# A sigmoid gate computed as one more column of a k projection and carried to its layout through DRAM

## The chip, the cores and the metric

The kernel runs on one core of a Trainium2 chip. The core has a matrix engine (TensorE, in the profile PE, with its weight loads as PEld), a vector engine (VectorE, DVE), an activation engine (ScalarE, ACT), a general engine (GpSimd, POOL) and a queue engine (SyncE, SP) that here only issues DMAs. The metric is the device time of one execution in microseconds, as the median of three runs.

## The reference

Two linear-attention blocks A and B, with weights of their own, read the same x (2048 rows, 640 columns, bf16). A gate mixes their outputs row by row:

```python
x = A_x
g = sigmoid((x * gate_w).sum(-1, keepdims=True))   # one number for each row of x
qkv = x @ wqkv                                      # 640 -> 3 * 640, 32 heads of 20
phi = lambda t: where(t > 0, t + 1, exp(t)) + 1e-6
pq, pk = phi(q), phi(k)
kv  = einsum("bhsd,bhse->bhde", pk, v);  z = einsum("bhsd->bhd", pk)
o   = einsum("bhqd,bhde->bhqe", pq, kv) / (einsum("bhqd,bhd->bhq", pq, z) + 1e-6)
a   = o @ wo            # and b in the same way with B's weights
out = g * a + (1 - g) * b
```

The gate's logit of a row is a dot product of that row with gate_w. With e the exponential of the logit, 1 / g is 1 + 1 / e and 1 / (1 - g) is 1 + e.

## The kernel before

The rows of x are cut into 16 chunks of 128 (ST = 16, half of them hc = 8), its 640 columns into 5 blocks of 128 (DT = 5). xT holds x transposed, xn holds x as it is. The first 512 rows come in by four loads and are transposed on PE (x_transpose, L207); the other 1536 rows are transposed by 15 DMA transposes on SP's queue (L155). DMAs are issued from SP and, for three blocks of x, one block of wkA and two late outputs, from ACT.

The program is written out by hand in the order in which each engine issues its work (`tc.manual_schedule`). The framework adds the waits between engines. PSUM tiles of the first stage go through four slots of two banks each, in turn.

In the first stage k of A is computed chunk by chunk: k_chunk (L258) multiplies a chunk of xT by wkA in two halves of 320 columns, 5 matmuls each, and k_done applies phi: an exponential on ACT (L225), a clamp on DVE (L230) and a combining operation on DVE that reads PSUM (L239). k_first (L265) does this for the first four chunks, interleaved with the transposes of x, so that work starts as blocks of x and of wkA land. The q projection comes in between as q_block and q_unit (L305), 10 matmuls of 512 columns each.

After the last k chunk q_pass (L743) runs the second half of q for A. Behind its first unit stands the gate's pass (gate_pass, L198): 40 matmuls of 256 columns. Its weights, gwr, are the gate column repeated 32 times, so that the logits appear in the layout of the denominators: 32 equal partitions for each of four groups of 256 rows, two halves side by side. ACT takes two exponentials of them (L204) and DVE adds one and clamps (L205): geA is 1 / g and geB is 1 / (1 - g). gate_w itself comes by a DMA of 640 single elements (gcol, L776). z_rows (L510) then sums pk over the rows.

rec_pass (L573) multiplies the denominators by ge on DVE and takes reciprocals (L582, L587). norm_spread (L623) spreads these over the heads by matmuls (exA), and q is scaled by them. So the gate reaches A's and B's q through the reciprocal. The rest of the kernel computes the summed products of pk and x (gs, gA), the same for B, and the outputs by Strassen-like products. The change doesn't touch it.

The program order of SP's queue matters: after the transposes it holds gcol, three loads of xn, wvA, woA and its rest, wkB (which goes to wkA's place and so waits until A's last k chunk is done), and wqB (which waits for A's last q).

```python
gate_pass()                                    # L747, behind the first q unit of the second half
in1=ge[b][:, part], op0=ALU.add, op1=ALU.mult  # L583, the gate's first use
k_chunk(0, ST - 2)                             # L789
nc.vector.tensor_copy(out=gwr[:], ...)         # L791
k_chunk(0, ST - 1)                             # L792
```

Of the kernel before, what the change touches and what calls it, by code (L numbers as in the profile page):

```python
# [8 lines left out]
P = 128  # L9
FP32 = mybir.dt.float32  # L10
BF16 = mybir.dt.bfloat16
# [5 lines left out]
DT = D // P  # L17
# [15 lines left out]
def kernel(  # L33
# [66 lines left out]
    ones = persist.tile([P, H], BF16, name="ones")  # L100
    gwr = persist.tile([P, DT, H], BF16, name="gwr")
    hc, ic = ST // 2, 2 * P
# [18 lines left out]
    )]  # L121
    ge = [persist.tile([P, 2 * RB], FP32, name=f"ge{b}") for b in "AB"]

# [10 lines left out]
    wq = [None, None]  # L134
    wk[0] = wpool.tile([P, DT, D], BF16, tag="wk", name="wkA")
    def load_x(eng, lo, hi):
        eng.dma_start(out=xn[:, lo:hi, :], in_=xb0[:, lo:hi, :])

    def load_wk(eng, lo, hi):
        eng.dma_start(out=wk[0][:, lo:hi, :], in_=wq_dram[0][:, lo:hi, D:2 * D])  # L140
# [10 lines left out]
    nc.sync.dma_start(out=wq[0][:], in_=wq_dram[0][:, :, 0:D])  # L151
    gcol = persist.tile([P, DT], BF16, name="gcol")
    for n in range(1, NB):
# [43 lines left out]

    def gate_pass():  # L198

        pt = ps("lg")  # L200
        for h in range(2):
            by_group(pt[:, 0, h * RB:(h + 1) * RB], gwr, xT, h)
        for b in range(2):
            nc.scalar.activation(out=ge[b][:], in_=pt[:, 0, :], func=ACT.Exp, scale=(-1.0, 1.0)[b])  # L204
            nc.vector.tensor_scalar(ge[b][:], ge[b][:], 1.0, 1e30, op0=ALU.add, op1=ALU.min)  # L205

    def x_transpose(i, slot, eng, cuts=(0, DT)):  # L207
        pt = ps_raw("xt", slot)
        for c in range(DT):
            nc.tensor.transpose(out=pt[:, c * P:(c + 1) * P], in_=xn[:, i, c * P:(c + 1) * P], identity=ident[:])  # L210
        copy = nc.scalar.copy if eng == "act" else nc.vector.tensor_copy
        src = pt[:, 0:D].rearrange("p (c n) -> p c n", c=DT)
        for lo, hi in zip(cuts, cuts[1:]):
            copy(out=xT[:, lo:hi, i * P:(i + 1) * P], in_=src[:, lo:hi])

    class Phi:
# [31 lines left out]

    def k_mm(b, i, c, pt, hf):
        nc.tensor.matmul(  # L250
            pt[:, hf, 0:HF], lhsT=xT[:, c, i * P:(i + 1) * P], rhs=wk[b][:, c, hf * HF:(hf + 1) * HF],
            start=(c == 0), stop=(c == DT - 1),
        )

    def k_done(b, i, pt):
        phi(pk[:, i, :].rearrange("p (b n) -> p b n", b=2), pt[:, :, 0:HF])

# [7 lines left out]
    def k_first():  # L265

        pts = [ps("kA", (2 + i) % 4) for i in (0, 1)]

        def part(i, cs):
            for c in cs:  # L270
                for hf in range(2):
# [12 lines left out]
        for i in range(3):  # L284
            part(i, (3, 4))
            k_done(0, i, pts[i])
        k_chunk(0, 3, 0)

# [284 lines left out]
    def rec_pass(b, zsel, slot):  # L573
# [5 lines left out]
        for h in range(2):  # L579
            part = slice(h * RB, (h + 1) * RB)  # L580
            d1 = work.tile([P, RB], FP32, tag="d1", name="d1")
            nc.vector.scalar_tensor_tensor(  # L582
                out=d1[:], in0=pt[:, 0, part], scalar=EPS, in1=ge[b][:, part], op0=ALU.add, op1=ALU.mult  # L583
            )
            rT = work.tile([P, RB], BF16, tag="rT", name="rT")
            with nc.allow_low_precision(reason="a fp32 reciprocal, stored as the bf16 that multiplies bf16"):
                nc.vector.reciprocal(out=rT[:], in_=d1[:])  # L587
            rts.append(rT)
# [173 lines left out]
    with tc.manual_schedule():  # L762
# [12 lines left out]
    with nc.allow_non_contiguous_dma(reason="640 elements, one to a partition and column"):  # L775
        nc.sync.dma_start(out=gcol[:], in_=gate_w.rearrange("(c p) -> p c", p=P))  # L776
    for n in range(1, NB):
# [4 lines left out]
    load_wo(0, nc.sync)  # L782
    wk[1] = load_w(1, "k", nc.sync)

# [3 lines left out]
    with tc.manual_schedule():  # L788
        k_chunk(0, ST - 2)  # L789
        turn[0] = (turn[0] + 1) % 4  # L790
        nc.vector.tensor_copy(out=gwr[:], in_=gcol[:, :, None].to_broadcast([P, DT, H]))  # L791
        k_chunk(0, ST - 1)  # L792
        k_sum(0, 1)
        zsel = q_pass([(m, 1) for m in range(DT)])
# [69 lines left out]

        scratch = ctx.enter_context(tc.tile_pool(name="scratch", bufs=1, space=bass.MemoryType.DRAM))
        m_rows = scratch.tile([D, D], BF16, name="m_rows")

# [144 lines left out]
```

## Time and profile before

| | |
|---|---|
| runs | 189.8, 189.89, 190.78 us; median 189.89 us |
| profiled execution | 191.16 us, its span 189.4 us, granted clock 1.0 |
| PE, PEld | 184.4 us (97%), 123.6 us (65%) |
| DVE, ACT, POOL | 156.0 us (82%), 86.7 us (46%), 8.6 us (5%) |
| chain: PE, DMA, DVE, ACT | 91%, 3%, 2%, 1% |
| DMA | 15.64 MB in 19759 packets |

The profile is one execution, and its times are positions in its span in microseconds. "L250" is line 250 of the kernel; a helper's line covers all its callers, so tile names tell more: kA is k of A in PSUM, lg the gate's logits, denA the denominators, d and rT their product with the gate and its reciprocal, exA the spread reciprocals. A row of the timeline gives start, length, engine, line, operation, what is written from what, shape and count, and in brackets how long the engine stood before it and for whom. The chain is the work that ended last, followed back. Rows of windows give, for a stretch, the busy time of each engine, then the clock, the DMA engines' share and GB/s.

### The profile page before, as it was taken

To read this page: it belongs to the slowest core of one execution; us is meant where nothing else is said; L and a number is where in the kernel's file an instruction comes from. 1 tells how busy PE (TensorE), PEld (TensorE's weight loads), DVE (VectorE), ACT (ScalarE), POOL (GpSimd) and SP (SyncE) were. 2 spreads that over 40 slices of the span, in tenths; PEclk is the share of its full clock that TensorE was granted. 3 is DMA by queue.
4 is the path that set the end of the run, shared out by engine and by line. 5 is a ranking of instruction groups with operands and counts; after the bars stand their busy time and mean duration, and the time that the engine had idled before them with its cause. 6 is when DMAs were issued, how large, how long until landed. Compare 5 with 4: busy or idle time off the path is not lost.

```text
span 189.4 us, 3688 instructions
## 1 busy us (share of the span) xinstructions
PE 184.4 (97%) x1494; PEld 123.6 (65%) x1494; DVE 156.0 (82%) x267; ACT 86.7 (46%) x134; POOL 8.6 (5%) x23
## 2 busy tenths in 40 slices
PE   8899999999999999999999999999999999999992
PEld 3566657766567677676666665767677776777771
DVE  1368968999898999998898987999997989787553
ACT  2055478544963351563959685662611611111110
POOL 8900000000000000000000000000000000000000
PEclk9999999999999999999999999999999999999999
DMA  6984439992040000005000000146600003213112
GB/s 181 321 147 88 105 61 315 324 194 106 3 143 31 3 0 0 0 3 165 8 3 2 0 0 0 29 137 214 146 0 3 0 3 108 99 39 106 69 69 71
DMA packets 19759, 15.64 MB, mean 83 GB/s; under 512 B 9502, under 2 KB 19614, under 8 KB 19742
## 3 DMA queue, kind: packets, MB, share of 16 engines
q1 hardware_dynamic: 18878, 14.59, 28.0%
q10 hardware_dynamic: 864, 0.82, 1.3%
q8 instruction: 11, 0.18, 0.4%
q14 instruction: 6, 0.05, 0.1%
HBM read 10.00 MB, written 3.44 MB: 71 GB/s over the span
## 4 chain that ended last, share of the span: by engine, by line
PE 91%; DMA 3%; DVE 2%; ACT 1%; ACTq 0%; issue 0%; DVEq 0%
PE gs L453 16%; PE qA L294 11%; PE kA L250 11%; PE kB L250 11%; PE q L348 7%; PE ox L653 6%; PE oy L653 5%; PE oz L653 5%; DMA xn<-in_A_x_dram 3%; PE ow L653 3%; PE gB L424 2%; PE gA L424 2%; PE qB L294 1%; PE q L294 1%; DVE osb L658 1%; PE mA L872 1%
## 5 line engine op out<-in xcount | busy, mean ns | idle before, releaser
L250 PEld LDWEIGHTS <-xT 128*128 128x128 bf16 x320 | 31.4, 99 | 15.0 <-issue 0.2
L230 DVE TENSOR_SCALAR e<-e 128x640 bf16<-128x640 bf16 (+2 forms) x56 | 19.3, 344 | 6.9 <-ACT e L225 6.7
L250 PE MATMUL kB<-wkB,xT 128*128 128x320 bf16 x160 | 24.2, 299 | 0.0
L250 PE MATMUL kA<-wkA,xT 128*128 128x320 bf16 x160 | 23.4, 306 | 0.0
L294 PE MATMUL qA<-xT,wqA 128*128 128x512 bf16 x100 | 22.4, 379 | 0.0
L294 PEld LDWEIGHTS <-wqA 128*128 128x128 bf16 x100 | 11.6, 118 | 9.3 <-issue 0.3
L225 ACT ACTIVATE e<-kA 128x640 bf16<-128x640 f32 x16 | 11.1, 704 | 13.3 <-PE kA L250 13.2
L453 PEld LDWEIGHTS <-xn 128*128 128x128 bf16 x128 | 12.2, 98 | 5.2 <-issue 0.5
L225 ACT ACTIVATE e<-kB 128x640 bf16<-128x640 f32 x16 | 11.3, 708 | 9.0 <-PE kB L250 8.9
L239 DVE SCALAR_TENSOR_TENSOR pk<-kA,e 128x640 bf16<-128x640 f32 x16 | 13.2, 824 | 1.7
L239 DVE SCALAR_TENSOR_TENSOR pk<-kB,e 128x640 bf16<-128x640 f32 x16 | 13.2, 823 | 1.5
L225 ACT ACTIVATE e<-qA 128x1024 bf16<-128x1024 f32 x10 | 10.2, 1024 | 8.6 <-PE qA L294 8.1
L697 ACT COPY u<-ox 128x320 f32<-128x320 f32 x8 | 3.4, 426 | 21.9 <-PE ox L653 21.9
L225 ACT ACTIVATE e<-q 128x512 bf16<-128x512 f32 x18 | 10.8, 598 | 5.4 <-PE q L348 3.8
L653 PEld LDWEIGHTS <-xT 128*128 128x128 bf16 x85 | 8.0, 98 | 3.0 <-DVE xT L592 0.2
L653 PEld LDWEIGHTS <-pqTA 128*128 128x128 bf16 x85 | 7.9, 98 | 2.9 <-issue 0.2
L653 PEld LDWEIGHTS <-pqTB 128*128 128x128 bf16 x80 | 7.8, 98 | 3.0
L453 PE MATMUL gs<-pk,xn 128*128 128x320 bf16 x64 | 9.5, 299 | 0.0
L348 PE MATMUL q<-xT,wqB 128*128 128x512 bf16 x32 | 9.5, 379 | 0.0
L658 DVE TENSOR_TENSOR osb<-oz,u 128x320 bf16<-128x320 f32 (+1 forms) x18 | 8.0, 452 | 1.6 <-PE oz L653 0.9
L424 PEld LDWEIGHTS <-xn 128*128 128x128 bf16 x64 | 6.3, 98 | 3.0 <-issue 0.4
L681 ACT COPY p1s<-ox 128x320 f32<-128x320 f32 x8 | 3.4, 426 | 10.0 <-PE ox L653 10.0
(145 smaller groups left out, 319.5 us busy)
## 6 DMA issues: line engine op xcount, KB each, us to landing
out_dram<-osb SPq DMA_DIRECT2D x14, 160.0 KB, 1.8
xn<-in_A_x_dram SPq DMA_DIRECT2D x3, 640.0 KB, 6.7
wqA<-in_A_wqkv_dram SPq DMA_DIRECT2D x1, 800.0 KB, 6.6
wvA<-in_A_wqkv_dram SPq DMA_DIRECT2D x1, 800.0 KB, 10.3
wkB<-in_B_wqkv_dram SPq DMA_DIRECT2D x1, 800.0 KB
wqB<-in_B_wqkv_dram SPq DMA_DIRECT2D x1, 800.0 KB, 4.5
wvB<-in_B_wqkv_dram SPq DMA_DIRECT2D x1, 800.0 KB, 4.5
MA<-m_rows SPq DMA_DIRECT2D x1, 800.0 KB, 4.5
```

The lines of the kernel that those rows point to most:

```text
L225: nc.scalar.activation(out=to, in_=part, func=ACT.Exp)
L230: nc.vector.tensor_scalar(self.e, self.e, 1.0, EPS, op0=ALU.min, op1=ALU.add)
L239: nc.vector.scalar_tensor_tensor(out=dst, in0=src, scalar=1.0 + EPS, in1=e, op0=ALU.add, op1=ALU.max)
L250: nc.tensor.matmul(pt[:, hf, 0:HF], lhsT=xT[:, c, i * P:(i + 1) * P], rhs=wk[b][:, c, hf * HF:(hf + 1) * HF], start=(c == 0), stop=(c == D ...
L294: nc.tensor.matmul(dst, lhsT=mixed(wq[b][:, c, :], m), rhs=xT[:, c, n * HB:(n + 1) * HB], start=first, stop=last,)
L348: nc.tensor.matmul(dst, lhsT=left(c), rhs=right(c), start=first and k == 0, stop=k == len(cs) - 1, skip_group_check=not first,)
L424: nc.tensor.matmul(pt[:, hf, 0:HF], lhsT=xn[:, i, c * P:(c + 1) * P], rhs=pk[:, i, hf * HF:(hf + 1) * HF], start=(i == 0), stop=(i == ST - 1),
L453: nc.tensor.matmul(pt[:, n, 0:HF], lhsT=left[:, i, n * P:(n + 1) * P], rhs=right[:, i, :], start=(first and i == 0), stop=(i == hc - 1), s ...
L653: nc.tensor.matmul(dst, lhsT=left[:, c, r0:r0 + P], rhs=right[:, c, :], start=(first and c == 0), stop=(c == DT - 1), skip_group_check=not ...
L658: nc.vector.tensor_tensor(out=dst, in0=acc, in1=sb, op=ALU.add)
L681: nc.scalar.copy(out=self.p1s[:], in_=self.at("x"))
L697: nc.scalar.copy(out=self.u2[:], in_=self.at("x"))
```

## The change

Four things change.

The gate's logits become a 641st column of A's k. wkA gets 642 columns, of which 640 are loaded as before. gate_w comes as 5 rows of 128 (g5), is transposed on PE into a free part of the PSUM tile of the second transposed chunk, and is copied by DVE into column 640 of each of the 5 blocks (gate_column). The second half of each of A's k chunks is then 321 columns wide, and k_done takes one more exponential on ACT, of that single column, into gl (128 partitions, 16 columns).

The gate's pass on PE, its two exponentials, its two DVE operations, gwr and gcol go. Instead gate_rows makes 1 + 1 / e and 1 + e for eight chunks at a time with three small DVE operations; gate_store writes them to a DRAM tile in row order, element by element, 2048 elements a time; gate_load reads them back, four DMAs a half, each to 32 partitions with the row repeated, into one tile ge for both blocks.

On SP's queue g5's load stands before wkA's third block; gcol is gone; wkB comes after the two stores and before the eight loads.

k_first has a new order: first-half products of chunk 0 for blocks 0 and 1, the gate's column, those of chunk 1, the second halves, both chunks' block 2 and only then the transpose of x's third block; the third and fourth chunks run as plain k chunks at the end.

```diff
+    g5 = persist.tile([DT, P], BF16, name="g5")
+    gl = persist.tile([P, ST], FP32, name="gl")
+    gf = persist.tile([P, 2, 2, ST // 2], FP32, name="gf")
...
-    ge = [persist.tile([P, 2 * RB], FP32, name=f"ge{b}") for b in "AB"]
+    ge = persist.tile([P, 2, 2 * RB], FP32, name="ge")
+    g_rows = [scratch.tile([2, SH], FP32, name=f"g_rows{h}") for h in range(2)]
...
-    wk[0] = wpool.tile([P, DT, D], BF16, tag="wk", name="wkA")
+    wk[0] = wpool.tile([P, DT, D + 2], BF16, tag="wk", name="wkA")
...
     load_wk(nc.scalar, 1, 2)
+    nc.sync.dma_start(out=g5[:], in_=gate_w.rearrange("(c p) -> c p", p=P))
     load_wk(nc.sync, 2, 3)
...
-    def gate_pass():
-        pt = ps("lg")
-        for h in range(2):
-            by_group(pt[:, 0, h * RB:(h + 1) * RB], gwr, xT, h)
-        for b in range(2):
-            nc.scalar.activation(out=ge[b][:], in_=pt[:, 0, :], func=ACT.Exp, scale=(-1.0, 1.0)[b])
-            nc.vector.tensor_scalar(ge[b][:], ge[b][:], 1.0, 1e30, op0=ALU.add, op1=ALU.min)
+    def gate_column(pt):
+        nc.tensor.transpose(out=pt[:, 2 * HB:2 * HB + DT], in_=g5[:], identity=ident[0:DT, 0:DT])
+        nc.vector.tensor_copy(out=wk[0][:, :, D:D + 1], in_=pt[:, 2 * HB:2 * HB + DT, None])
+
+    def gate_rows(h):
+        cols = slice(h * ST // 2, (h + 1) * ST // 2)
+        nc.vector.tensor_scalar(gf[:, h, 1], gl[:, cols], 1e-30, 1e30, op0=ALU.max, op1=ALU.min)
+        nc.vector.reciprocal(out=gf[:, h, 0], in_=gf[:, h, 1])
+        nc.vector.tensor_scalar(gf[:, h], gf[:, h], 1.0, 1e30, op0=ALU.add, op1=ALU.min)
+
+    def gate_store(h):
+            nc.sync.dma_start(out=g_rows[h].rearrange("b (i p) -> p (b i)", p=P), in_=gf[:, h].rearrange("p b i -> p (b i)"))
+
+    def gate_load(h):
+        for j in range(4):
+            nc.sync.dma_start(
+                out=ge[32 * j:32 * j + 32, :, h * RB:(h + 1) * RB],
+                in_=g_rows[h][None, :, j * RB:(j + 1) * RB].to_broadcast([H, 2, RB]),
+            )
...
     def k_mm(b, i, c, pt, hf):
+        n = HF + (b == 0 and hf == 1)
         nc.tensor.matmul(
-            pt[:, hf, 0:HF], lhsT=xT[:, c, i * P:(i + 1) * P], rhs=wk[b][:, c, hf * HF:(hf + 1) * HF],
+            pt[:, hf, 0:n], lhsT=xT[:, c, i * P:(i + 1) * P], rhs=wk[b][:, c, hf * HF:hf * HF + n],
...
     def k_done(b, i, pt):
-        phi(pk[:, i, :].rearrange("p (b n) -> p b n", b=2), pt[:, :, 0:HF])
+        f = Phi(pk[:, i, :].rearrange("p (b n) -> p b n", b=2), pt[:, :, 0:HF])
+        if b == 0:
+            nc.scalar.activation(out=gl[:, i:i + 1], in_=pt[:, 1, HF:HF + 1], func=ACT.Exp)
+        f.clamp()
+        f.top()
...
         for i in range(2):
-            x_transpose(i, i, "dve", (0, 2, DT))
+            pt = x_transpose(i, i, "dve", (0, 2, DT))
+        part(0, (0, 1), (0,))
+        gate_column(pt)
+        part(1, (0, 1), (0,))
         for i in range(2):
-            part(i, (0, 1))
-        x_transpose(2, 0, "dve", (0, 2, DT))
+            part(i, (0, 1), (1,))
         for i in range(2):
             part(i, (2,))
-        pts.append(ps("kA", 1))
-        part(2, (0, 1, 2))
-        x_transpose(3, 0, "dve")
-        for i in range(3):
-            part(i, (3, 4))
+        x_transpose(2, 0, "dve", (0, 2, DT))
+        part(0, (3, 4))
+        x_transpose(3, 1, "dve", (0, 2, DT))
+        part(1, (3, 4))
+        for i in range(2):
             k_done(0, i, pts[i])
-        k_chunk(0, 3, 0)
+        for i in (2, 3):
+            k_chunk(0, i, i - 2)
...
-                out=d1[:], in0=pt[:, 0, part], scalar=EPS, in1=ge[b][:, part], op0=ALU.add, op1=ALU.mult
+                out=d1[:], in0=pt[:, 0, part], scalar=EPS, in1=ge[:, b, part], op0=ALU.add, op1=ALU.mult
...
         q_unit(0, *units.pop(0))
-        gate_pass()
         zr = z_rows(0)
...
-        nc.sync.dma_start(out=gcol[:], in_=gate_w.rearrange("(c p) -> p c", p=P))
...
-    wk[1] = load_w(1, "k", nc.sync)
...
         k_chunk(0, ST - 2)
         turn[0] = (turn[0] + 1) % 4
-        nc.vector.tensor_copy(out=gwr[:], in_=gcol[:, :, None].to_broadcast([P, DT, H]))
+        gate_rows(0)
+        gate_store(0)
         k_chunk(0, ST - 1)
+        gate_rows(1)
+        gate_store(1)
+        wk[1] = load_w(1, "k", nc.sync)
+        for h in range(2):
+            gate_load(h)
         k_sum(0, 1)
```

More of the change, by code (lines that the diff above doesn't have):

```diff
@@ L121 @@
     )]
-    ge = [persist.tile([P, 2 * RB], FP32, name=f"ge{b}") for b in "AB"]
+    ge = persist.tile([P, 2, 2 * RB], FP32, name="ge")
+    scratch = ctx.enter_context(tc.tile_pool(name="scratch", bufs=1, space=bass.MemoryType.DRAM))
+    m_rows = scratch.tile([D, D], BF16, name="m_rows")
+    g_rows = [scratch.tile([2, SH], FP32, name=f"g_rows{h}") for h in range(2)]
     wq_dram = [A_wqkv.rearrange("(c p) f -> p c f", p=P), B_wqkv.rearrange("(c p) f -> p c f", p=P)]
@@ L139, in load_wk @@
     def load_wk(eng, lo, hi):
-        eng.dma_start(out=wk[0][:, lo:hi, :], in_=wq_dram[0][:, lo:hi, D:2 * D])
+        eng.dma_start(out=wk[0][:, lo:hi, 0:D], in_=wq_dram[0][:, lo:hi, D:2 * D])
     load_x(nc.sync, 0, 1)
@@ L196, in by_group @@
                 )
-    def gate_pass():
-        pt = ps("lg")
-        for h in range(2):
-            by_group(pt[:, 0, h * RB:(h + 1) * RB], gwr, xT, h)
-        for b in range(2):
-            nc.scalar.activation(out=ge[b][:], in_=pt[:, 0, :], func=ACT.Exp, scale=(-1.0, 1.0)[b])
-            nc.vector.tensor_scalar(ge[b][:], ge[b][:], 1.0, 1e30, op0=ALU.add, op1=ALU.min)
+    def gate_column(pt):
[7 more added lines that the diff above has]
+    def gate_store(h):
+        with nc.allow_non_contiguous_dma(reason="a row of x to a partition and column"):
+            nc.sync.dma_start(out=g_rows[h].rearrange("b (i p) -> p (b i)", p=P), in_=gf[:, h].rearrange("p b i -> p (b i)"))
[5 more added lines that the diff above has]
+            )
     def x_transpose(i, slot, eng, cuts=(0, DT)):
@@ L214, in x_transpose @@
             copy(out=xT[:, lo:hi, i * P:(i + 1) * P], in_=src[:, lo:hi])
+        return pt
     class Phi:
@@ L267, in k_first, with part @@
         pts = [ps("kA", (2 + i) % 4) for i in (0, 1)]
-        def part(i, cs):
+        def part(i, cs, hfs=(0, 1)):
             for c in cs:
-                for hf in range(2):
+                for hf in hfs:
                     k_mm(0, i, c, pts[i], hf)
         for i in range(2):
-            x_transpose(i, i, "dve", (0, 2, DT))
+            pt = x_transpose(i, i, "dve", (0, 2, DT))
+        part(0, (0, 1), (0,))
+        gate_column(pt)
+        part(1, (0, 1), (0,))
         for i in range(2):
-            part(i, (0, 1))
-        x_transpose(2, 0, "dve", (0, 2, DT))
+            part(i, (0, 1), (1,))
         for i in range(2):
             part(i, (2,))
-        pts.append(ps("kA", 1))
-        part(2, (0, 1, 2))
-        x_transpose(3, 0, "dve")
-        for i in range(3):
-            part(i, (3, 4))
+        x_transpose(2, 0, "dve", (0, 2, DT))
[3 more added lines that the diff above has]
+        for i in range(2):
             k_done(0, i, pts[i])
-        k_chunk(0, 3, 0)
+        for i in (2, 3):
+            k_chunk(0, i, i - 2)
     def mixed(t, m):
@@ L774 @@
                 sq_sum(4, 0)
-    with nc.allow_non_contiguous_dma(reason="640 elements, one to a partition and column"):
-        nc.sync.dma_start(out=gcol[:], in_=gate_w.rearrange("(c p) -> p c", p=P))
     for n in range(1, NB):
```

4 lines of the change are left out of this document (removed).

## The prediction, made before the result was known

> **What bounds the kernel now.** I read the page's first part, the chain, the start of PE's timeline, the DVE rows before the first use of the gate, and the DMA rows of the one load made of single elements.
>
> Part 1 of the page:
> ```profile
> PE 184.4 (97%) x1494; PEld 123.6 (65%) x1494; DVE 156.0 (82%) x267; ACT 86.7 (46%) x134; POOL 8.6 (5%) x23
> ```
> PE is busy 97% of the span, so an instruction taken off PE is worth its length, if nothing that PE waits for becomes late. The chain in order of time:
> ```profile
> 1.73 5.91 DMA xn<-in_A_x_dram
> 7.69 0.45 PE xt L210 x5
> 8.14 1.38 PE kA L250 x10
> ...
> 39.87 2.16 PE qA L294 x10
> 42.03 1.21 PE lg L193 x39
> 43.24 1.09 PE zA L516 x32
> ...
> 59.80 1.20 PE denA L193 x40
> 61.01 4.45 PE gs L453 x32
> 65.46 0.33 PE exA L629 x8
> ```
> Look at two places: lg, the gate's own pass, lies on the chain at 42.03 with 1.21 us, and the chain begins with a load of x that lands at 7.64. PE's timeline there:
> ```profile
> 5.01 2.13 PE L250 MATMUL kA<-wkA,xT 128*128 128x320 bf16 x8
> 7.69 0.45 PE L210 MATMUL xt<-ident,xn 128*128 128x128 bf16 x5 [0.54 <-DMA xn<-in_A_x_dram]
> ```
> PE stands for 0.54 us. DVE where the gate is first used:
> ```profile
> 61.06 0.42 DVE L582 SCALAR_TENSOR_TENSOR d<-denA,geA 128x256 f32<-128x256 f32 x1 [0.42 <-PE denA L193]
> 61.52 1.75 DVE L587 RECIPROCAL rT<-d 128x256 bf16<-128x256 f32 x1
> 63.19 0.36 DVE L582 SCALAR_TENSOR_TENSOR d<-denA,geA 128x256 f32<-128x256 f32 x1
> 63.59 1.75 DVE L587 RECIPROCAL rT<-d 128x256 bf16<-128x256 f32 x1
> ```
> DVE waits 0.42 us for denA, then needs until 65.34, and exA on PE starts at 65.46: 0.12 us of slack. Whatever makes d late makes PE late. The DMA answer and the windows around the load of gate_w (columns at the end: clock, DMA share, GB/s):
> ```profile
> gcol<-in_gate_w_dram SPq DMA_DIRECT2D x1, 1.2 KB, 4.2
> ```
> ```profile
> 27.00:27.50 0.50, 0.50 (x4) 0.25 (x3) 0.48 (x1) 0.50 (x1) 0.00 (x0) 1.00 0.15 1
> 28.00:28.50 0.50, 0.50 (x4) 0.30 (x3) 0.50 (x2) 0.50 (x1) 0.00 (x0) 1.00 0.15 1
> 28.50:29.00 0.50, 0.50 (x5) 0.25 (x4) 0.50 (x2) 0.41 (x1) 0.00 (x0) 1.00 0.51 75
> ```
> 1.2 KB in single elements holds the queue: 1 GB/s, although the loads of xn behind it were issued from 26.30. In the trace's packet records its 640 packets of 2 bytes start between 27.0 and 29.5, so 40 per DMA engine, one in 62 ns.
>
> **The change, part by part.**
> *Gate pass off PE:* 40 matmuls, -1.21 us on the chain. zA follows directly; it needs the last pk only in its last 8 matmuls, 0.8 us in, and pk ends at 41.93 now, about 42.2 then. Cover holds. Slots turn by one: gA now takes the slot of the fourth q unit, which ACT leaves at 53.19 (52.08 + 1.11), against gA at 53.28: 0.09 of cover, 0 to 0.05 lost.
>
> *The 641st column:* 80 matmuls go from 320 to 321 columns. L250's pace is 1.36 us / 10 = 136 ns, or 0.42 ns a column: +0.03 us. Rows of wkA now start off round addresses; kvA's right operands do too (slices from multiples of 120 columns) and 35 of them took 1.87 us, 53 ns for up to 120 columns, the same pace. Nothing for that.
>
> *ACT:* 16 exponentials of 128x1. From 597 ns (512 wide) and 1024 ns (1024) a line leaves 0.17 us at width zero, so 16 x 0.17 = 2.7 us, less the two of 0.6 us. ACT waits 0.65 us for PE in each k chunk, which hides 0.17. Behind gl stands only the next chunk's exp. Without that cover each would cost 0.17.
>
> *DVE:* gwr's copy (0.31) and two ge operations (0.42 each, 0.67 together by starts) go. Two gate_rows of three small operations come. A 40x40 mask took 0.18, memset of one column 0.06, a reciprocal costs 1.75 / 256 = 7 ns an element: 0.15 each, bounds 0.06 and 0.25, 0.5 us a group. The first replaces gwr's copy, +0.2 ahead of the last pk; the second stands before k_sum. Adding up DVE's starts from 41.85 on with ACT's and PE's waits moved up by 1.21, DVE is ready for d at about 60.1, denA ends at 61.01 - 1.21 = 59.8. So some 0.2 us of the gain is lost at exA (0 to 0.4): +0.2.
>
> *Front:* the two c = 2 steps (4 matmuls, 4 x 138 ns = 0.55) now stand before the transpose of x's third block and fill the 0.54 wait; added are one 5-column transpose of g5 and a column copy on DVE behind the xT copies (5.76). From 7.2, eight matmuls as before, the 5.09 us that stood between 7.69 and 12.78 follow without a gap: 12.35. Gain 0.40. What is late next: wkA's last rows, wanted at 8.3 instead of 9.8; the packet records have that queue's first 640 packets (x's first block and wkA) started by 6.8, so they are there. g5 is issued before wkA's third block, one more SP issue (0.42-0.46 us); the 160 KB behind it took 4.4 us to land at 6.1, mostly queueing, and is wanted at 7.2. One more early DMA also makes x's fourth block, on ACT's queue, the ninth; the ninth DMA before (wqA) waited 1.4 us for x's first to land (3.91). So ACT's queue stands until 4.0, its table load (1.28) ends at 5.4, before the first exp at 8.9; the block itself queues behind the third, landing at 7.64. Bounds: 0.54 gained, 0.5 lost (rival three). -0.40.
>
> *DMA path of the gate:* gcol's load goes, so xn, wvA and woA run 2 us earlier and the queue is empty at 40. Then, less the 0.4 of the front: first store issued 40.6, packets from 41.6 (issue to first packet was 0.85 us for the last output, 1.1 for gcol). Each store is 2048 elements of 4 bytes, 128 per engine, T us. Both stores run one behind the other, then wkB (2.2 us at its 380 GB/s, issued 39.90 before, now behind them), then four loads of 64 KB (0.7) and landing (0.5): ge's first half at 45.0 + 2T. SP waits at the loads for the stores; behind it is only wqB, wanted at 75.4, and wkB, wanted at 74.6: 15 us of room. d wants the half at 60.1 - 0.4 = 59.7; the second half 2.1 us later. So T may be 7.3 us, 57 ns an element.
> T is in no row. Above: gcol's 62 ns, T = 8.0, ge late by 1.3. Below: the last 80 KB outputs, 128 packets of 640 bytes started within 0.32 us, 40 ns an engine's packet, T = 5.1. The store shares its direction with the outputs and its grain with gcol; gcol's engines were busy 0.15 of the time, waiting between reads of 2 bytes from DRAM, which the store doesn't make. I take the middle, 51 ns, T = 6.5, ge at 58.0: no wait, 0 us.
>
> *Sum:* -1.21 - 0.40 + 0.03 + 0.20 = -1.38 us. The profiled execution took 191.16 (span 189.4 and 1.7 around it), 1.3 above the median 189.89; the stretches come from the span, so I take them off the median: 188.5.
>
> [...]
>
> **Rivals.**
> *One, the stores run at gcol's pace (55 to 66 ns).* T = 7.0 to 8.5, ge late by 0 to 2.3, d, the reciprocals and exA with it, one for one. At 62 ns: 188.5 + 1.3 = 189.8. For it: the same grain; against it: no DRAM reads.
> *Two, slower: writes of 4 bytes cost more than gcol's reads.* Place: SP's queue, then d at L582. From T = 8.5 it outweighs both gains. At 80 ns T = 10.2, late by 5.7, 194.2; at 124 ns, twice gcol's, T = 15.9, 17 us late, 206. For it: neighbouring partitions write neighbouring 4-byte words of 8 KB. Against it: 640-byte packets into DRAM go at 40 ns. [...]
> *Three, the front backfires:* the column's copy on DVE waits for g5 or for wkA's last rows (7.2), the second-half matmuls behind it, and PE resumes at 7.6 with 36 matmuls and two blocks of transposes, 5.7 us: 13.3, 0.5 late instead of 0.4 early: 189.4. For: PE has only hf = 0 work until the column is there. Against: DVE copied into xT at 4.67 while DMA transposes wrote its other columns, so regions are told apart.
>
> **How the numbers follow.** Forecast (ge in time) 0.47, own range 187.9 (front 0.54, no DVE loss, and scatter) to 189.0; rival one 0.18; two 0.27; three 0.08. Half a per cent, 0.95 us, is about what a measurement tells from no change. Faster: 0.46 of the forecast and 0.02 of rival one, 0.48. Same: 0.13 of one, 0.08 of three, 0.01: 0.22. Slower: 0.27 of two and 0.03 of one, 0.30. The range goes from 187.9 to 195.0, T = 10.6, which leaves out the upper half of rival two and little below.
>
> **What would show it.** zA directly behind the first q unit; first q unit at 12.4 instead of 12.78; no wait of PE at 7.2; d at L582 idle before it by denA or not at all, against "DMA ge"; the stores' landing 7 to 8 us after issue for the first. Wrong if DVE waits for ge, if exA's PE start is more than 4.6 us after denA's end, or if kA matmuls wait in the first 8 us.

## The result, and the profile after

The kernel got slower: 200.09 us median (199.27 to 201.15), against 189.87 for the kernel before beside it, a ratio of 1.053 (95%: 1.049 to 1.057). The forecast of 188.5 and its range up to 195.0 were wrong. What happened is nearest to rival two, the slow writes of 4 bytes, and the time lies between its two prices (194.2 and 206). The profiled execution took 200.02 us, its span 198.3.

The page of the kernel after, its first and second parts:

```profile
PE 186.5 (94%) x1455; PEld 123.7 (62%) x1455; DVE 156.4 (79%) x272; ACT 86.8 (44%) x148; POOL 8.6 (4%) x23
...
PEclk9999999999999856999999999999999999999999
```

The last of these rows in the kernel before:

```profile
PEclk9999999999999999999999999999999999999999
```

PE has 39 instructions less and is busy 2.1 us longer, and the granted clock, flat in every slice before, dips in the slices from 64 to 79 us. The chain of the kernel after:

```profile
3.95 3.91 DMA wkA<-in_A_wqkv_dram
8.89 3.27 PE kA L271 x24
12.17 4.32 PE qA L322 x20
...
42.89 23.50 DMA wkB<-in_B_wqkv_dram
66.41 2.03 DMA ge<-g_rows
68.48 1.39 issue
70.27 1.76 DVE rT L615
72.48 11.51 PE gs L481 x64
83.99 2.72 PE kB L271 x20
```

From 42.89 to 68.44, where PE carried the chain before, there is now DMA. (The 1.39 us of "issue" behind it are no stand: DVE is busy with the reciprocal of the first half, from 68.20 to 69.95.) PE's timeline around it, and DVE's first use of the gate:

```profile
39.18 2.32 PE L322 MATMUL qA<-xT,wqA 128*128 128x512 bf16 x10
41.43 1.27 PE L544 MATMUL zA<-pk,ones 128*32 128x320 bf16 x32
...
58.23 1.28 PE L198 MATMUL denA<-pqTA,zsel 128*32 128x256 bf16 x40
...
70.38 0.40 PE L657 MATMUL exA<-rT,spread 32*128 32x256 bf16 x4 [6.42 <-DVE d L610]
72.08 0.40 PE L657 MATMUL exA<-rT,spread 32*128 32x256 bf16 x4 [1.29 <-DVE rT L615]
```
```profile
67.74 0.42 DVE L610 SCALAR_TENSOR_TENSOR d<-denA,ge 128x256 f32<-128x256 f32 x1 [8.06 <-DMA ge<-g_rows]
```

Up to denA the change does what it was said to do: zA follows the q unit directly, and denA starts at 58.23, 1.50 us earlier than before (59.73 in the timeline). DVE is ready for d at 67.74 - 8.06 = 59.68. Then d waits 8.06 us for ge, and PE stands 6.42 + 1.29 us. The queue of SP (its last four loads once more by themselves), the landing times of the DMA answer, and windows (clock, DMA share and GB/s are the last three columns), all of the kernel after:

```profile
40.70 2.10 SPq L217 DMA_DIRECT2D g_rows<-gf  x2
42.89 0.90 SPq L760 DMA_DIRECT2D wkB<-in_B_wqkv_dram  x1
59.36 7.35 SPq L221 DMA_DIRECT2D ge<-g_rows  x8
```
```profile
63.33 3.38 SPq L221 DMA_DIRECT2D ge<-g_rows  x4
```
```profile
ge<-g_rows SPq DMA_DIRECT2D x8, 64.0 KB, 7.3
g_rows<-gf SPq DMA_DIRECT2D x2, 8.0 KB, 18.6
```
```profile
48.00:52.00 4.00, 4.00 (x20) 2.15 (x19) 3.90 (x6) 3.54 (x5) 0.00 (x0) 1.00 1.36 11
...
68.00:72.00 4.00, 0.40 (x4) 0.14 (x5) 3.93 (x5) 0.00 (x0) 0.00 (x0) 0.50 0.65 205
72.00:76.00 4.00, 3.92 (x18) 2.20 (x18) 4.00 (x5) 1.93 (x2) 0.00 (x0) 0.50 0.02 4
```

The first store is issued when the prediction said (40.70), but lands 18.6 us later, and the first load of ge can only be issued at 59.36. The answer gives the landing of the first store alone; the second one, issued at 42.41, holds up the fifth load, the first of the second half, until 63.33.

The trace's packet records show the 4-byte packets starting much sooner: up to 851 in half a microsecond, half of the 4096 by 43 us, nearly all by 49 and the last by 51.0. So all of them had started some 8 us before even the first store had landed. Of wkB's 640 packets of 1280 bytes, which start between 48.9 and 65.6, 406 took under 0.1 us (55 ns as a rule), but 166 took over 0.4 us, up to 4.1. The windows show engines that are busy by the profile's measure (share 1.36) and move 11 GB/s. In the kernel before, a window full of loads looks like this:

```profile
40.00:44.00 4.00, 4.00 (x78) 2.67 (x80) 3.79 (x7) 2.35 (x4) 0.00 (x0) 1.00 0.87 237
```

The sum of the two executions: 1.50 us ahead at denA; then gs behind exA starts 6.69 us late (65.79 on the chain before, 72.48 now): 7.71 of stands and some 0.5 for exA, whose matmuls took 0.80 us instead of 0.33, less the 1.50 that had been gained. Its 64 matmuls took 8.80 us before and 11.51 now, as the clock is at 0.50 in the two windows from 68 to 76 (by the trace's clock records from 67.7 to 78.0): 2.71 us more, 9.40 at kB. The tail gives 0.5 back: 8.9, the difference of the spans.

### The profile page after: what moved, and what is told of

Read it like the earlier page. It is cut to its first block, busy times and chain, and to the rows that moved or that the text cites. A ratio compares the mean times of both kernels' runs of the same rounds, so it can differ in the third digit from the quotient of the medians.

```text
span 198.3 us, 3651 instructions
## 1 busy us (share of the span) xinstructions
PE 186.5 (94%) x1455; PEld 123.7 (62%) x1455; DVE 156.4 (79%) x272; ACT 86.8 (44%) x148; POOL 8.6 (4%) x23
## 4 chain that ended last, share of the span: by engine, by line
PE 69%; DMA 16%; DVE 9%; issue 2%; ACT 1%; DVEq 0%; SPq 0%; ACTq 0%
PE gs L481 14%; DMA wkB<-in_B_wqkv_dram 12%; PE kB L271 10%; PE q L376 7%; PE ox L681 6%; PE qA L322 5%; PE oy L681 5%; PE oz L681 5%; PE kA L271 5%; DVE pk L259 3%; PE ow L681 2%; PE gB L452 2%; DMA wkA<-in_A_wqkv_dram 2%; DMA xn<-in_A_x_dram 2%; DVE e L250 1%
## 5 line engine op out<-in xcount | busy, mean ns | idle before, releaser
L271 PE MATMUL kA<-wkA,xT 128*128 128x320 bf16 (+1 forms) x160 | 23.3, 303 | 0.1
L481 PEld LDWEIGHTS <-xn 128*128 128x128 bf16 x128 | 13.0, 104 | 6.3 <-issue 0.5
L481 PEld LDWEIGHTS <-S 128*128 128x128 bf16 x64 | 6.4, 103 | 3.2 <-issue 0.4
L452 PEld LDWEIGHTS <-xn 128*128 128x128 bf16 x64 | 6.2, 98 | 3.1 <-issue 0.7
```

Source lines behind the costliest of these rows:

```text
L271: nc.tensor.matmul(pt[:, hf, 0:n], lhsT=xT[:, c, i * P:(i + 1) * P], rhs=wk[b][:, c, hf * HF:hf * HF + n], start=(c == 0), stop=(c == DT - 1),
L452: nc.tensor.matmul(pt[:, hf, 0:HF], lhsT=xn[:, i, c * P:(c + 1) * P], rhs=pk[:, i, hf * HF:(hf + 1) * HF], start=(i == 0), stop=(i == ST - 1),
L481: nc.tensor.matmul(pt[:, n, 0:HF], lhsT=left[:, i, n * P:(n + 1) * P], rhs=right[:, i, :], start=(first and i == 0), stop=(i == hc - 1), s ...
```

## The experiments

All ratios are to the kernel before on the same chip, with 95% intervals. "Landing" is the median from a DMA's issue to its end, over those whose end the profile tells; of the two stores that is in some runs the first alone, and the text says so.

**Is it the writes themselves, or wkB in their way?**

```diff
         gate_store(1)
-        wk[1] = load_w(1, "k", nc.sync)
         for h in range(2):
             gate_load(h)
+        wk[1] = load_w(1, "k", nc.sync)
```

> The changed kernel with wkB's load issued behind the gate's eight loads instead of between stores and loads; nothing else differs. In the changed kernel the stores landed 18.6 us (first) and about 21 us (second) after 40.70 and 41.6, the loads 7.3 us after issue, and d waited 8.06 us. Theory A (the 4-byte writes themselves take some 18 us to land, whoever is behind them): the first store lands at about 59.3 again, ge's first half at 61.5 instead of 67.7, the second at about 65.5; d waits 2 us for the first half and 1.5 to 2 for the second, PE stands under 4 us and its clock does not fall: 192 us, between 190.5 and 194. Theory B (wkB in front of the loads is what makes ge late): ge is there by 59.7, no wait, 188.3 us. Theory C (wkB's reads slow the stores' writes down, as they share the queue): the stores land much sooner than 59.3, at 50 to 54, no wait, 188.3 us; the stores' own landing tells B from C.

Measured: 196.77 us, 1.033 (1.028 to 1.038). SP's queue and the DMA answer of this kernel:

```profile
41.60 2.10 SPq L217 DMA_DIRECT2D g_rows<-gf  x2
58.37 6.92 SPq L221 DMA_DIRECT2D ge<-g_rows  x8
```
```profile
ge<-g_rows SPq DMA_DIRECT2D x8, 64.0 KB, 6.4
g_rows<-gf SPq DMA_DIRECT2D x2, 8.0 KB, 16.7
```

With no large load behind them the first store still needs 16.7 us, so it is the writes (theory A so far); the second was in by 63.57, where the fifth load of ge goes out. wkB in the way adds some 3.3 us to the whole (200.09 - 196.77, which were not measured side by side). The time is above the expectation, because the eight small loads take 6.4 us too, d waits 5.52 us, and the clock falls to 0.50 here as well.

**Elements or places?** First, the same bytes into the same 8 KB in pieces of 64 bytes:

```diff
-  out=g_rows[h].rearrange("b (i p) -> p (b i)", p=P)
+  out=g_rows[h].rearrange("b s -> (b s)").rearrange("(p n) -> p n", p=P)
```

> The changed kernel with the same 8 KB of each store laid down as 16 neighbouring fp32 numbers of each partition, 64 bytes in one piece, 128 packets in place of 2048; the order of the rows in DRAM is then not that of x, so the gate's values go to wrong rows: this kernel leaves out the bringing into row order. Theory A (the grain of 4 bytes is what lands late): the stores land about 2 us after issue, wkB at its usual rate, ge's halves by 50, no wait at d: 188.2 to 188.6 us. Rival (the way through DRAM with a wait of SP for the landing and eight loads behind wkB is too long in itself): d still waits, over 190 us.

Then single elements again, but each 64 bytes from the next:

```diff
+    g_wide = scratch.tile([2, 2, SH, 16], FP32, name="g_wide")
-  out=g_rows[h].rearrange("b (i p) -> p (b i)", p=P)
+  out=g_wide[h, :, :, 0].rearrange("b (i p) -> p (b i)", p=P)
```

> The changed kernel with the same 4-byte writes, each of them 64 bytes from the next instead of 4, into a DRAM tile that was filled beforehand; the loads read 1 KB rows of that tile, so most of what they bring is the filling: this kernel leaves out the right gate values and keeps the writes, the waits and the loads' sizes. Theory A (a 4-byte write is slow by itself): the first store lands 15 to 20 us after issue again, the time is within 1.5 us of the changed kernel's 200.1. Rival D (writes are slow because 16 of them, from neighbouring partitions and different DMA engines, fall into the same 64 bytes): the stores land 3 to 9 us after issue, ge is in time, 188.3 us.

Measured: 189.54 us, 0.9955 (0.9929 to 0.9981), and 189.46 us, 0.9964 (0.9942 to 0.9986). The DMA answers, pieces of 64 bytes first:

```profile
ge<-g_rows SPq DMA_DIRECT2D x8, 64.0 KB, 4.8
g_rows<-gf SPq DMA_DIRECT2D x2, 8.0 KB, 1.4
```
```profile
ge<-g_wide SPq DMA_DIRECT2D x8, 64.0 KB, 5.0
g_wide<-gf SPq DMA_DIRECT2D x2, 8.0 KB, 6.8
```

As many 4-byte writes as in the kernel after land in 5.0 us (first store) and 8.7 (second) when they don't meet in the same 64 bytes, d waits for nothing, and the kernel is a little faster than before. So theory A falls as it stood: 4-byte writes are dearer than pieces of 64 bytes (1.4 us), but the greater part of the cost comes with where they fall (D). The spread stores also touch 128 KB instead of 8 KB (g_wide, which one more store, not shown, fills beforehand; the first gate store goes out behind that, at 43.13), and each 64 bytes has one writing partition instead of 16. Two runs took these apart.

**Many writers, small region, or the same 64 bytes?** Single elements into 8 KB, but each partition's 16 into 64 bytes of its own:

```diff
-  nc.sync.dma_start(out=g_rows[h].rearrange("b (i p) -> p (b i)", p=P), ...)
+  for b in range(2):
+      nc.sync.dma_start(
+          out=g_rows[h].rearrange("b s -> (b s)").rearrange("(p i b) -> p i b", p=P, b=2)[:, :, b],
+          in_=gf[:, h, b])
```

> The kernel after, whose stores still write single 4-byte elements into the same 8 KB a half, but each partition writes 16 elements into 64 bytes of its own (two stores a half, one for each of the two gate forms, each with every second word), where the kernel after spreads neighbouring 4 bytes over neighbouring partitions. The rows are not in their order, so gates meet other rows. It tells apart what the spread stores left open. Theory F, the cost comes from 16 partitions, whose packets run on several DMA engines, writing into the same 64 bytes: each 64 bytes has one writer here, the stores land in 1.4 to 7 us, d does not wait, 189.5 us. Theory G, it comes from many 4-byte writes into the same 64 bytes, whoever writes, or from so many writes into only 8 KB: nothing is changed, landing 14 to 19 us, d waits 6 to 8 us, 197 to 200 us. In between (landing 8 to 12 us, 190 to 194) would say that both the number of writers and the number of writes count. Before: 190.2.

And the same with these 64 bytes 1 KB apart, in a g_wide that is filled beforehand as in store_spread:

```diff
+          out=g_wide[h].rearrange("b s w -> (b s w)").rearrange("(p n) -> p n", p=P)[:, b:16:2],
```

> store_own_line with one thing changed: the 64 bytes that a partition writes with 16 elements stand 1 KB from those of the next partition, so 128 KB a half are touched instead of 8 KB, as in store_spread; the loads read 1 KB rows of the same 256 KB tile, prefilled, so the gates are not the ones just written. Theory of the line: the cost is many 4-byte writes into the same 64 bytes; nothing is changed against store_own_line, landing 11 to 19 us, time 196 to 200. Theory of the region: it is 2048 writes into only 8 KB, and 128 KB take them as store_spread's did; landing 5 to 7 us, no wait of d, 189.5. In between, landing 7 to 10 us and 189.5 to 193, both count.

Measured: 199.87 us, 1.049 (1.045 to 1.054), and 206.02 us, 1.080 (1.075 to 1.085). SP's queue and the stores of the DMA answer in the first and in the second (four stores now, of 1024 writes each):

```profile
40.85 2.94 SPq L218 DMA_DIRECT2D g_rows<-gf  x4
...
55.30 11.77 SPq L224 DMA_DIRECT2D ge<-g_rows  x8
```
```profile
g_rows<-gf SPq DMA_DIRECT2D x4, 4.0 KB, 11.7
```
```profile
41.56 2.26 SPq L218 DMA_DIRECT2D g_wide<-gf  x4
...
60.87 11.27 SPq L224 DMA_DIRECT2D ge<-g_wide  x8
```
```profile
g_wide<-gf SPq DMA_DIRECT2D x4, 4.0 KB, 10.4
```

One writer for each 64 bytes doesn't help: 14.4 us from the first store's issue to the first load's. Nor does a region of 128 KB: 19.3 us. store_spread, with the region of the second and one write for each 64 bytes, needed 43.13 to 48.15, 5.0 us, for the same 2048 writes. Even the first store by itself, of 1024 writes, landed only after 9.7 and 10.4 us. Of what was tried, it is left that 16 writes fall into the same 64 bytes. No other distance than 64 bytes and no number between 1 and 16 was tried, so the size of the piece that counts isn't shown. That own_line_apart is slower still, by 6 us, wasn't followed up.

**Does it cost when nobody reads?** The kernel before, with the two stores added and wkB behind them:

```diff
+        nc.vector.memset(gf[:], 2.0)
         k_chunk(0, ST - 1)
+        for h in range(2):
+            nc.sync.dma_start(out=g_rows[h].rearrange("b (i p) -> p (b i)", p=P), in_=gf[:, h]...)
+        wk[1] = load_w(1, "k", nc.sync)
```

> The kernel before, its gate pass kept, with the two element stores of a constant issued on SP where the change has them, wkB's load behind them, and nobody who reads or waits for them. Theory A (all of the loss is the wait of d, with PE's clock after it): no change, 189.9 us within 0.5, with wkB landing at about 64 to 67, before its use at 74.6. Rival E (the writes also slow what the engines read and write in SBUF, or later loads): slower by over 1 us, 191 or more.

Measured: 190.46, 193.59, 195.29 and 195.77 us, where 19 runs of the kernel before on this chip gave 189.58 to 191.19. One run shows no loss and three show 2.4 us and more; no interval is given for runs so far apart, and neither theory is decided. The chain of the one that was profiled (195.77):

```profile
61.15 3.77 PE gs L457 x27
64.92 2.63 issue
67.55 1.52 PE gs L457 x5
69.61 9.48 PE gs L457 x64
```

PE stands 2.63 us in the middle of its matmuls for nothing that the profile shows. The packet records show one thing that fits: a 16 KB packet of the queue that the page calls "q8 instruction" (11 packets, 0.18 MB), which comes at 47.6 us in the kernel before, comes here only at 65.1, when wkB has drained, and at 64.8 in the kernel after. That PE stood for want of instructions is the author's estimate from these times, not shown.

**Can the stores go early enough?** First store as soon as its half is there, second as before, all large loads behind ge's:

```diff
+            if i == hc + 2:
+                gate_rows(0)
...
+    gate_store(0)
...
         for h in range(2):
             gate_load(h)
+        wk[1] = load_w(1, "k", nc.sync)
+        wv[0] = load_w(0, "v", nc.sync)
+        load_wo(0, nc.sync)
```

> The changed kernel with its way through DRAM kept and the order on SP's queue changed: the first half's gate rows are made after the eleventh k chunk and stored behind the loads of xn; wkB, wvA and woA are all loaded behind the gate's loads. If a store of 2048 elements alone lands within 10 us, the first lands at about 44, the second, issued at 42.4, by 53, ge is there by 56, no wait: 188.3 us. If 18 us is the time of one store and not of two, the second lands at 60, the second half of ge at 62, when d asks for it at 61.8: 188.3 to 189. Rival: the late loads of wkB, wvA and woA miss their uses (74, 83): over 190.

Measured: 190.79 us, 1.002 (0.9995 to 1.005). The first store, alone on the queue for 6.5 us, goes at 36.45, its packets have all started by 39.0, and the first load goes at 50.73, 14.3 us after the store. d waits only for denA (0.58). So all of the loss can be bought off by issuing earlier; no gain is left (188.3 expected), and PE stands 0.96 us for wkA's last rows.

**The layout without DRAM.** The column stays; 16 matmuls against the identity spread the logits over the partitions instead of stores and loads:

```diff
+        for i in range(ST):
+            h, j, u = i // 8, i % 8 // 2, i % 2
+            nc.tensor.matmul(pt[32 * j:32 * j + 32, 0, h * RB + u * P:h * RB + (u + 1) * P],
+                lhsT=gl[:, i:i + 1].to_broadcast([P, H]), rhs=ident[:], ..., tile_position=(0, 32 * j))
```

> The logits as the 641st column, but brought to the gates' layout by PE: ACT copies the column as bf16 logits to SBUF, and where the gate's pass stood 16 matmuls of 128 columns (the chunk's column repeated 32 times as weights, the identity as right operand) write the logits into the layout, with the two exponentials and two DVE operations of before behind them. No DRAM. Theory (all of the loss is the way through DRAM): PE loses the 40 matmuls of 256 columns (1.21 us) and gains 16 of 128, some 0.25 to 0.5 us, the front gives 0.6: 188.3 to 188.7 us, faster than before by 0.6 to 0.8%. Rival (weights with one column repeated are slow to load, or DVE is late at d): 189.5 or more.

**The front alone.** The kernel before with the new order of k_first and nothing else of the change:

```diff
-            part(i, (0, 1))
-        x_transpose(2, 0, "dve", (0, 2, DT))
+            part(i, (0, 1), (1,))
         for i in range(2):
             part(i, (2,))
+        x_transpose(2, 0, "dve", (0, 2, DT))
```

> The kernel before with the new order of the first four k chunks alone: no gate column, no load of the column, the gate's pass and everything else as before. From the changed kernel's trace, where the first q unit started at 12.17 instead of 12.78, the front is worth 0.6 us: 189.3, between 189.2 and 189.6. Rival (the gain came from the blocks of x landing sooner in that one execution, not from the order): 189.9.

Measured: pe_layout 190.33 us, 1.0007 (0.9989 to 1.0025); front_alone 190.43 us, 1.0006 (0.9987 to 1.0024). PE's timeline in front_alone:

```profile
7.85 0.70 PE L250 MATMUL kA<-wkA,xT 128*128 128x320 bf16 x4 [0.88 <-DMA wkA<-in_A_wqkv_dram]
```

The wait for x of the kernel before (0.54) is gone, and one of 0.88 us for wkA's last rows stands in its place. In pe_layout it is 0.46, ahead of a first q unit at 12.27 in the timeline; its pass takes 0.35 us instead of 1.21, and no gain can be measured. Both runs miss the gain that was expected of them (189.3, and 188.3 to 188.7).

**Rows of 512 bytes.** By the finding on the 64 bytes, the gate's way through DRAM should work with long pieces. One matmul against the identity turns the 128 x 16 logits into 16 x 128, and the exponentials follow there:

```diff
+        nc.tensor.matmul(pt[0:ST, 0, 0:P], lhsT=gl[:], rhs=ident[:], start=True, stop=True)
+        for b in range(2):
+            nc.scalar.activation(out=gr[0:ST, b * P:(b + 1) * P], in_=pt[0:ST, 0, 0:P], func=ACT.Exp, scale=(-1.0, 1.0)[b])
+        nc.vector.tensor_scalar(gr[0:ST], gr[0:ST], 1.0, 1e30, op0=ALU.add, op1=ALU.min)
+        nc.sync.dma_start(out=g_rows.rearrange("b (i n) -> i b n", n=P), in_=gr[0:ST]...)
```

> The kernel after with rows of 512 bytes instead of elements: gl keeps the logits (copies on ScalarE, bf16), one matmul against the identity behind the first q unit turns the 128 x 16 logits into 16 x 128, two exponentials and one operation on VectorE make both gate forms there, and one store of 32 pieces of 512 bytes takes them to DRAM; then wkB and the same eight loads. By theory D the writes no longer meet in the same 64 bytes: landing 1.5 to 2.5 us, the first half of the gates at about 50, wanted at 59.7, no wait of d. The PE pass of 1.21 us is replaced by one matmul (0.06 to 0.2). Sum against before: -1.21 + 0.15 + 0.09 (column) + 0.22 (late pk and the slot of the fourth q unit) = -0.75, so 189.5, if the front is as in the kernel before; with the wait for wkA's last rows (0.5) 190.0. If writes into few DRAM lines were slow by their number alone, 32 pieces could not show it and the time is the same; if loads behind any store were slow, d waits 2 to 6 us and the time is 193 or more.

Three variants of its front. g5 behind wkA's last load:

```diff
-    nc.sync.dma_start(out=g5[:], ...)
     load_wk(nc.sync, 2, 3)
...
     load_wk(nc.sync, 3, DT)
+    nc.sync.dma_start(out=g5[:], ...)
```

> row_store with the load of g5 behind wkA's last load instead of ahead of wkA's third block. Theory of the ninth DMA: with g5 ahead, wkA's last load is the ninth and its issue waits for x's first block (1.4 us), so PE waits 0.5 to 0.9 for wkA's last rows. Here g5 is the ninth and wkA's last load goes out some 1.8 us earlier: no wait for wkA, but g5 lands only at about 5.5 to 6.5 and the gate's column, wanted at 5.8, may make PE wait up to 0.7 of its own. First q unit at 11.7 to 12.1 against 12.5, time 0.3 to 0.5 below row_store. Rival: the rows land late because 16 engines are busy, not because the issue is late; then the first q unit stays at 12.4 to 12.6 and the time is that of row_store.

wkA's blocks 2 to 4 in one load:

```diff
-    load_wk(nc.sync, 2, 3)
     load_x(nc.scalar, 2, 3)
-    load_wk(nc.sync, 3, DT)
+    load_wk(nc.sync, 2, DT)
```

> row_store with wkA's third, fourth and fifth blocks in one load behind g5, so that no early DMA is the ninth but x's fourth block on ScalarE's queue. Theory of the ninth DMA: the issue at 2.1 doesn't wait, all three blocks land at about 6.5 to 7.2; block 2, wanted at 7.2, comes with the others; no wait of PE for wkA above 0.3, first q unit at 11.9 to 12.2 and time 0.3 to 0.5 below row_store. Rival (the engines are busy): PE waits 0.5 or more for wkA and the time is that of row_store.

The old order of k_first, but for the split of the first two blocks into halves:

```diff
             part(i, (0, 1), (1,))
+        x_transpose(2, 0, "dve", (0, 2, DT))
         for i in range(2):
             part(i, (2,))
-        x_transpose(2, 0, "dve", (0, 2, DT))
-        part(0, (3, 4))
-        x_transpose(3, 1, "dve", (0, 2, DT))
-        part(1, (3, 4))
-        for i in range(2):
+        pts.append(ps("kA", 1))
+        part(2, (0, 1, 2))
+        x_transpose(3, 0, "dve")
+        for i in range(3):
+            part(i, (3, 4))
             k_done(0, i, pts[i])
-        for i in (2, 3):
-            k_chunk(0, i, i - 2)
+        k_chunk(0, 3, 0)
```

> row_store with the order of k_first as in the kernel before, but for the two halves of the first two blocks (first halves, the gate's column, second halves). wkA's last rows are then wanted at about 9.8 instead of 8.3. Theory: the front's gain was given back because the order wants wkA's last rows at 8.0 and they land at 7.9 to 8.9 in all kernels with that order; with the old order PE waits 0.5 for x's third block and not for wkA, first q unit at 12.2 to 12.6, time 0.3 to 0.7 below row_store and 0.5 to 0.7% below the kernel before. Rival: x's third and fourth blocks are late by as much as wkA's rows, as the 16 engines share what they move; PE waits over 1 us for xn, first q unit at 12.8 to 13.2, no gain over row_store.

| kernel | median us | ratio (95%) |
|---|---|---|
| row_store | 189.51 | 0.9967 (0.9941 to 0.9993) |
| row_store_g5_late | 192.64 | 1.0101 (1.0041 to 1.0161) |
| row_store_wk_merged | 190.87 | 1.0046 (1.0014 to 1.0078) |
| row_store_old_front | 189.51 | 0.9950 (0.9932 to 0.9969) |

PE's timeline, DVE's first use of the gate and the DMA answer of row_store_old_front:

```profile
11.62 3.62 PE L323 MATMUL qA<-xT,wqA 128*128 128x512 bf16 x15
...
41.47 0.22 PE L210 MATMUL lg<-ident,gl 128*16 128x128 bf16 x1
...
63.84 0.40 PE L658 MATMUL exA<-rT,spread 32*128 32x256 bf16 x8
```
```profile
59.51 0.42 DVE L611 SCALAR_TENSOR_TENSOR d<-denA,ge 128x256 f32<-128x256 f32 x1 [0.42 <-PE denA L197]
```
```profile
ge<-g_rows SPq DMA_DIRECT2D x8, 64.0 KB, 4.0
g_rows<-gr SPq DMA_DIRECT2D x1, 16.0 KB, 1.4
```

The store lands in 1.4 us, d waits for denA and no longer for ge, and both row_store kernels are a little faster than the kernel before, by 0.3% and 0.5%, with intervals that leave out 1. One matmul of 0.22 us stands where the pass took 1.21, and the stretch from the first q unit to exA in the timeline is 63.84 - 11.62 = 52.22 us against 65.39 - 12.62 = 52.77 in the kernel before.

The variants of the front went against their theory. In row_store PE stood 1.35 us for wkA, with its load issued only after a wait for x's first block. With g5 behind it wkA is in time, but g5 lands at 7.4 and PE stands 1.78 us for it (0.7 expected), and the ten matmuls behind that stand took 2.85 us against 1.59 in row_store. Merged, no load waits, and wkA's rows still land at 7.9 (PE stands 1.38). The runs of these two spread by 2 us and more, and the spread goes with the granted clock: the five merged runs from 192.0 to 192.4 were granted 0.991 of it on average, the other seven, from 190.3 to 191.0, 0.997 or more. So when the load is issued is one part; that the other is how much the 16 engines have to move by then is the author's estimate (in the kernel after their share is 0.96 to 0.98 from 2 to 8 us), and which of the two decides in an execution stays open. The old order, which wants these rows later, stood for none of them in its profile. Its median is that of row_store, and the two were measured on different chips, so a gain from the order alone isn't shown.

## Why the prediction was wrong, and where it was right

*Gate pass off PE, -1.21:* right. zA starts where the q unit ends. denA's start adds up: -0.61 (first q unit at 12.17 instead of 12.78), -1.21 and some 0.3 of small losses give -1.50.

*The column, +0.03, and the cover of zA and gA, 0 to 0.05:* a little short. In store_64b, whose gate path is quiet, the k chunks lost 0.09 in all, zA 0.11 (it waits for the last pk) and gA 0.11 (for its slot): 0.31 where 0.03 to 0.08 stood.

*ACT and DVE:* right. The exponentials took 0.17 each, the three operations of gate_rows 0.16, 0.20 and 0.17 (0.15 taken), and DVE was ready for d at 59.68 (59.7 forecast). The 0.20 of loss at exA didn't come: from denA to exA store_64b needs 5.65 us, the kernel before 5.66.

*Front, -0.40:* wrong as a lasting gain. The failing step is the one on wkA's last rows: their packets had started by 6.8, "so they are there". Started isn't landed: wkA's last rows land at 7.86 in the chain of after and PE stood for them in front_alone. In the kernel after this load was also issued at 3.95 instead of 2.19, behind a wait of 1.4 us for x's first block. So the ninth early DMA, which here waited for the first, was wkA's last load on SP's queue and not x's fourth block on ACT's, as the prediction had it. The wait that was to be filled was partly a matter of that one execution, too: store_alone, with the same front as the kernel before, had its first q unit at 11.88 instead of 12.78. That the profiled execution lay 1.3 us above the median should have been a warning to count nothing that only it shows.

*DMA path, 0, from T = 6.5 us:* this decided. The step that failed is the time of the store: it was priced at 51 ns an element, from the pace at which packets start, and was to land 7 to 8 us after its issue. The first store landed after 18.6. By the formula, ge at 45.0 + 2T, the measured 67.74 is T = 11.4, 89 ns an element, inside rival two's span of 80 to 124. But the formula itself was built on the packets' pace, and that wasn't the limit: both stores' packets had all started by 51.0 us, sooner than even the lower bound of 40 ns (5.1 us a store from 41.6, so 51.8) had it, and the first landing came 8 us later. What stood behind the stores was mis-sized with them: 2.2 us for wkB, which came 23.5 us after its issue, and 0.7 + 0.5 for the loads, which took 7.3. No row of before had many small writes to neighbouring addresses; gcol's reads and the outputs' writes of 640 bytes, the two ends of the range, both missed the thing that mattered. Rival two did name it ("neighbouring partitions write neighbouring 4-byte words of 8 KB"), with a chance of 0.27. That the time fell between its prices is in part luck, as they go by the same pace and hold no clock. Two readings of the packet records are a little off without moving the sum: the 128 packets of an 80 KB output start within 0.35 to 0.38 us (43 to 48 ns an engine's packet), and gcol's first comes 1.3 us after its issue.

*The price of a write, in rival two:* its direction was right. But its upper price takes an element at 124 ns, twice gcol's, and no run shows that doubling. The runs put the price elsewhere: pieces of 64 bytes land in 1.4 us (store_64b), as pieces of 512 bytes do (row_store), and single writes of 4 bytes in 5.0 us when each has 64 bytes of its own (store_spread). Most of the cost comes where 16 writes fall into the same 64 bytes (14.3 us for one store in stores_first). What the engines or the memory do there, no run shows.

*What no step had:* the clock. A late ge was priced one for one: 188.5 + 8.06 = 196.6. The half clock added 2.71 on gs and some 0.5 on exA, 199.7, against 200.09 measured. The granted clock fell to 0.50 at 67.7, 3.8 us after PE's last matmul. It also fell 3.0 us after PE's last matmul in wkb_last, 2.1 in store_own_line, and behind a stand of 2.63 us in store_alone, so these runs give no one length of stand at which it falls. The prediction's rivals that end in a long wait should each have carried that price.

*wkB:* its cover held. It came 23.5 us after its issue, at 66.4, and before the change its first use was at 74.6.

## What to carry to other kernels

When a layout goes through DRAM, look at how many separate writes fall into the same 64 bytes, not at the bytes or at the pace of the packets: turn the data first, even with a matmul, so that each row is written in one piece (here 14.3 us for 2048 writes of 4 bytes with 16 to each 64 bytes, 5.0 with one, and 1.4 for rows of 512 bytes). From a trace, take the time at which a transfer landed (who waited for it, and until when), not the time at which its packets started. Price a stall of PE of several microseconds above its length (behind the 6.42 us here the clock stood at 0.50 and 64 matmuls took 2.71 us more), and don't count as a gain a wait that one profiled execution alone shows.

## What the runs showed of the hardware that was not expected

- 2048 writes of 4 bytes, 16 to each 64 bytes, landed 14.3 us after issue in stores_first, though their packets had all started within 2.6 us of it. With a second such store 1.7 us behind, into other 64 bytes, the first landed after 16.7 (wkb_last) and both were in 22.0 us after the first's issue (41.60 to 63.57). So twice the writes took about half as long again: the two go side by side in part. The order of the writes within 64 bytes wasn't varied.
- Loads behind such writes were slow. wkB, 800 KB, took 23.5 us to land, where wqB, a load of the same size, took 4.5 us in the kernel before. The loads of 64 KB took 7.3 us, and 6.4 without wkB (wkb_last), instead of 4.0 in row_store_old_front.
- After PE's stand of 6.42 us the granted clock was 0.50 for 10.24 us, which cost 2.71 us on 64 matmuls. In the other profiles in which the clock fell behind a stand of PE the clock records give 3.41 us (store_alone), 6.83 (wkb_last), 10.24 (store_own_line) and 13.65 (own_line_apart): whole multiples of 3.41.
